# 56 matmuls on half and full rows of the array added behind the preparation of the first keys

## The chip, the cores and the metric

One Trainium2 chip, one core of it in use. The time is device microseconds of one execution of the whole program, from the start to the end of the kernel on that core; the median of several runs is compared.

## The reference

Three stages run one after the other, in fp32, on batch 2, 3008 rows and 256 columns:

```python
scores = (1.0 / S) * np.matmul(z, z.transpose(0, 2, 1))   # z: 2 x 3008 x 64
attn = np.maximum(scores, 0.0) ** 2
x = (u * np.matmul(attn, v)).reshape(B * S, D)            # u, v: 2 x 3008 x 256
h = x @ w_in                                              # 256 -> 2048
P = a[0] + a[1] * h + a[2] * h**2 + a[3] * h**3
Q = 1.0 + np.abs(b[0]) * np.abs(h) + np.abs(b[1]) * h**2
x = (P / (Q + 1e-06)) @ w_out                             # 2048 -> 256
h = x @ w_in2
out = np.maximum(0.01 * h, h) @ w_out2
```

The weights of the first pair arrive as 64-bit floats and are converted on the chip; those of the second pair likewise.

## The kernel before

The 6016 rows are cut into 12 blocks (`blocks`), six for each batch, of 512 query rows (448 in the last of a batch). Attention goes over the keys in pairs of 128: `NPAIR` = 12 steps for a block, 144 steps in all. One step `t` is four matmuls of scores (`scores`, L243), two ScalarE passes (ReLU L245, square L246), two VectorE passes that split the result into a high and a low half (L251, L256), and, two steps later (`DEPTH`), twelve matmuls with the values (`av`, L275). Each tensor that a matmul reads is held as a high part and a low remainder, both in the fp32r form, so that sums of products keep fp32 accuracy. The score matmul uses this in the partition direction: the 64 columns of z are laid twice on the 128 partitions of a key tile, the high part on partitions 0 to 63 and the remainder on 64 to 127.

The order of the work on every engine is the order in which the program issues it (`tc.manual_schedule()`); each engine's queue is in order. `tasks` holds what is issued at which step; step -1 is run ahead of the loop over `t`. In it stand, in this order, the loads of the first 1024 keys (two halves, on SP's and ScalarE's DMA queues), the load of an activation table, `first_z`, and the load and preparation of the first values (`prep_v`, L200 and L201).

`first_z` (L169 to L184) transposes eight tiles of z on TensorE into two PSUM tiles (`pf`, of the tag `acc1`, and `pg`, of the tag `big`, which has two buffers) and makes from them:

- `queries[0]`, a tile of 128 x 2 x 512: plane 0 is the rounded z (L178), plane 1 the remainder (L182);
- `key_chunk(0)`, a tile of 128 x 1024: the rounded half on partitions 0 to 63 (L181 for columns 0 to 511, L183 for 512 to 1023), the remainder on partitions 64 to 127 (L180 and L184).

Behind it TensorE's queue goes on with `scores(0)`, `scores(1)`, the eight transposes of the second 1024 keys (`prep_z`, L153, whose raw data comes by DMA from L129), `scores(2)`, `av(0)`, `scores(3)`, `av(1)` and so on, one `scores` and one `av` in turn. `av(0)` takes the PSUM tile of the tag `acc0`; nothing ahead of it uses that tag.

Each matmul of the program is two instructions on TensorE, a load of 128 x 128 weights and the stream of the moving operand; the trace lists them as PEld and PE.

Of the kernel before, what the change touches and what calls it, by code (L numbers as in the profile page):

```python
# [17 lines left out]
def f32(ap):  # L18
    return ap.bitcast(F32)
# [3 lines left out]
def squared_relu_attention_moe_moe2(  # L23
# [14 lines left out]
    pe, act, dve, pool, sp = nc.tensor, nc.scalar, nc.vector, nc.gpsimd, nc.sync  # L38
# [4 lines left out]
    P = 128  # L43
# [24 lines left out]
    def big(name):  # L68
        return ps.tile([P, 2, QB], F32, tag="big", name=name)

    def acc(k, name):
        return ps.tile([P, 2, QB], F32, tag=f"acc{k}", name=name, bufs=1)
# [4 lines left out]
    def idle_acc(i, name):  # L77
        return acc(1 - own_acc(i), name)
# [39 lines left out]
    queries = [sb.tile([P, 2, QB], F32R, tag="sq", name="sq"), keys[1][:, 1, :].rearrange("p (a b) -> p a b", a=2)]  # L118
# [3 lines left out]
    def key_chunk(c):  # L122
        return keys[c // 2][:, c % 2, :]

    def load_z(b, c, k0=0, k1=8):
        t = raw_slot(f"zraw{b}_{c}_{k0}", (P, 8, 2, DQ))
        f0, f1 = c * 8 + k0, min(c * 8 + k1, S // P)
        for d, queue in enumerate((sp, act if c == 0 else sp)):
            queue.dma_start(t[:, : f1 - f0, d, :], z[b, f0 * P : f1 * P, :].rearrange("(k p) d -> p k d", p=P))  # L129
        if f1 - c * 8 < k1:  # L130
            for h in range(2):
                for d in range(2):
                    sp.dma_start(t[h * KTAIL : (h + 1) * KTAIL, f1 - f0, d, :], z[b, f1 * P : S, :])
        return t
# [16 lines left out]
    def turn_z(pf, t, n):  # L151
        for k in range(n):
            pe.transpose(pf[:, k * P : (k + 1) * P], t[:, k, :, :].rearrange("p a d -> p (a d)"), ident)  # L153
# [15 lines left out]
    def first_z(ts):  # L169
        pf = idle_acc(0, "zT0_0").rearrange("p a b -> p (a b)")  # L170
        pg = big("zT0_0b").rearrange("p a b -> p (a b)")
        m, q = key_chunk(0), queries[0]
        for _ in range(WARM):
            pe.matmul(pg[:, :P], ident, ident, start=True, stop=True)
        turn_z(pf, ts[0], 4)
        for _ in range(2):
            pe.matmul(pg[:, QB : QB + P], ident, ident, start=True, stop=True)
        act.activation(q[:, 0, :], pf[:, :QB], AF.Copy)  # L178
        turn_z(pg, ts[1], 4)
        dve.tensor_tensor(out=m[64:, :QB], in0=pf[64:, :QB], in1=f32(q[64:, 0, :]), op=ALU.subtract)  # L180
        act.activation(m[:64, :QB], f32(q[:64, 0, :]), AF.Copy)  # L181
        dve.tensor_tensor(out=q[:, 1, :], in0=pf[:, :QB], in1=f32(q[:, 0, :]), op=ALU.subtract)  # L182
        act.activation(m[:, QB:], pg[:, :QB], AF.Copy)  # L183
        dve.tensor_tensor(out=m[64:, QB:], in0=pg[64:, :QB], in1=f32(m[64:, QB:]), op=ALU.subtract)  # L184

    def load_v(b, c):
        t = raw_slot(f"vraw{b}_{c}", (P, 4, D))
        k0 = c * 4
        full = min(4, S // P - k0)
        sp.dma_start(t[:, :full, :], v[b, k0 * P : (k0 + full) * P, :].rearrange("(k p) d -> p k d", p=P))  # L190
        if full < 4:
            for h in range(2):
                sp.dma_start(t[h * KTAIL : (h + 1) * KTAIL, full, :], v[b, (k0 + full) * P : S, :])
        return t

    def prep_v(b, c, t):
        m = rtile(3 + c, f"V{b}_{c}")
        V[b, c] = m
        tf = t.rearrange("p k d -> p (k d)")
        act.activation(m[:, 0, :], tf, AF.Copy)  # L200
        dve.tensor_tensor(out=m[:, 1, :], in0=tf, in1=f32(m[:, 0, :]), op=ALU.subtract)  # L201
        if c == KB // 4 - 1:
            o = 3 * D
            act.activation(m[:KTAIL, 1, o:], f32(m[:KTAIL, 0, o:]), AF.Copy)
            pool.memset(f32(m[KTAIL:, 0, o:]), 0.0)
# [145 lines left out]
    def at(step, f):  # L351
        tasks.setdefault(step, []).append(f)
# [3 lines left out]
    def prep(step, lead, key, load, use):  # L356
        at(step - lead, lambda: held.__setitem__(key, load()))
        at(step, lambda: use(held.pop(key)))

    def zt(b, c, step, lead):  # L360
        prep(step, lead, ("z", b, c), lambda: load_z(b, c), lambda t: prep_z(b, c, t, step // NPAIR))

    def zs(b, c, step, lead):
        key = "z", b, c
        at(step - lead, lambda: held.__setitem__(key, load_z_squares(b, c)))
        at(step, lambda: dve.transpose(out=held[key], in_=held[key]))
        at(step + 1, lambda: round_z(c, held[key]))
        at(step + 2, lambda: lower_z(c, held.pop(key)))

    def vt(b, c, step, lead):  # L370
        prep(step, lead, ("v", b, c), lambda: load_v(b, c), lambda t: prep_v(b, c, t))

    NV, NM = KB // 4, KB // 8
    for b in range(B):
        s0 = b * NQ * NPAIR
        if b == 0:
            at(-1, lambda: held.__setitem__("z", [load_z(0, 0, k, k + 4) for k in (0, 4)]))
            at(-1, lambda: act.preload_act_table_set("natural_log_exp_and_others"))
            at(-1, lambda: first_z(held.pop("z")))
            vt(0, 0, -1, 0)  # L380
            zt(0, 1, 1, 2)
            vt(0, 1, 2, 3)
            for c in range(2, NV):
                vt(0, c, 2 * c, 3)
            zs(0, 2, 3, 3)
        else:
            for c in range(NM):
                zs(b, c, s0 + (-8, -4, 3)[c], (13, 11, 3)[c])
            for c in range(NV):
                vt(b, c, s0 - NPAIR + 2 * c + 4, (14, 14, 3, 3, 3, 3)[c])  # L390
# [336 lines left out]
```

## Time and profile before

| what | value |
|---|---|
| median of 2 runs | 1552.22 us (1551.65 and 1552.78) |
| span of the profiled execution | 1550.2 us, first to last instruction |
| TensorE matmul busy | 1542.4 us, 99% of the span |
| weight loads busy | 1297.8 us |
| VectorE busy | 1367.6 us, 88% |
| ScalarE busy | 1067.2 us, 69% |

The profiled execution is given by its span alone; its time is this span and what lies ahead of the first instruction and behind the last, which by the median of the runs is 2.0 us. Busy time of PE is the union of the matmuls' durations, which overlap one another, so a busy PE isn't PE at its peak; the distance between the starts of consecutive matmuls tells more.

### The profile page before, as it was taken

What the parts mean: (1) busy time and instruction counts of PE and PEld (TensorE: products, weight loads), DVE (VectorE), ACT (ScalarE), POOL (GpSimd) and SP (SyncE); (2) the same over time, 40 slices, a digit from 0 to 9 for tenths busy, and PEclk for the clock granted to TensorE, in tenths of its full rate; (3) what the DMA queues carried; (4) which work ended last, traced back from release to release, by engine and by line L of the source; (5) the groups of instructions that cost most, each with busy time, mean ns of one, the idle gap of its engine ahead of it and who ended that gap; (6) DMA issues with size and microseconds to landing.
All of it is one profiled execution on the core that took longest, in us unless ns stands there. A gap on an engine that the chain in (4) does not pass through costs nothing.

```text
span 1550.2 us, 17531 instructions
## 1 busy us (share of the span) xinstructions
PE 1542.4 (99%) x6920; PEld 1297.8 (84%) x6920; DVE 1367.6 (88%) x1301; ACT 1067.2 (69%) x1072; POOL 1.4 (0%) x10
## 2 busy tenths in 40 slices
PE   9999999999999999999999999999999999999998
PEld 7888889888888888888888888888888888888888
DVE  7888889788789899999999998999999999999862
ACT  7666667766677767777667677677776676767653
POOL 0000000000000000000000000000000000000000
PEclk9999999999999999999999999999999999999999
DMA  7332456355410340000000010000000000100001
GB/s 188 84 80 71 108 135 173 82 130 142 109 39 1 121 152 10 14 14 14 14 12 15 1 28 1 14 14 14 13 14 14 14 14 1 22 5 1 14 8 19
DMA packets 144978, 74.41 MB, mean 48 GB/s; under 512 B 121344, under 2 KB 128512, under 8 KB 143872
## 3 DMA queue, kind: packets, MB, share of 16 engines
q1 hardware_dynamic: 141984, 72.80, 18.7%
q8 instruction: 55, 0.90, 0.3%
q10 hardware_dynamic: 2912, 0.49, 0.2%
q14 instruction: 27, 0.22, 0.0%
HBM read 46.93 MB, written 20.71 MB: 44 GB/s over the span
## 4 chain that ended last, share of the span: by engine, by line
PE 97%; DVE 2%; DMA 0%; ACT 0%; issue 0%; SPq 0%; DVEq 0%
PE h L456 33%; PE y L467 32%; PE oT L275 24%; PE sc L243 8%; PE y2b L467 1%; DMA zraw<-in_z_dram 0%; DVE t L499 0%; DVE t L498 0%; DVE pl L256 0%; DVE t L494 0%; DVE t L518 0%; DVE gh L510 0%; DVE t L514 0%; DVE ph L251 0%; SPq L129 0%
## 5 line engine op out<-in xcount | busy, mean ns | idle before, releaser
L467 PE MATMUL y<-gh,w 128*128 128x512 f32 (+1 forms) x1504 | 370.3, 386 | 0.2 <-ACT gh L541 0.2
L467 PEld LDWEIGHTS y<-gh,w 128*128 128x128 f32 x1504 | 282.3, 188 | 53.7 <-ACT gh L541 0.6
L275 PE MATMUL oT<-ph,V 128*128 128x512 f32 (+1 forms) x1128 | 274.7, 385 | 0.0
L275 PEld LDWEIGHTS oT<-ph,V 128*128 128x128 f32 x1128 | 211.7, 188 | 39.8
L467 PE MATMUL y<-gl,w 128*128 128x512 f32 (+1 forms) x752 | 200.1, 386 | 0.1
L484 ACT ACTIVATE t<-h,par 128x1024 f32<-128x1024 f32 (+1 forms) x91 | 100.2, 1101 | 134.9 <-PE h L456 134.9
L541 ACT ACTIVATE gh<-h 128x1024 fp32r<-128x1024 f32 (+1 forms) x96 | 97.0, 1010 | 131.0 <-PE y L467 109.7
L456 PE MATMUL h<-x2h,w 128*128 128x512 f32 (+1 forms) x768 | 186.6, 385 | 0.0
L456 PEld LDWEIGHTS h<-x2h,w 128*128 128x128 f32 x768 | 144.2, 188 | 26.5
L467 PEld LDWEIGHTS y<-gl,w 128*128 128x128 f32 x752 | 141.1, 188 | 27.5 <-DVE gl L548 0.5
L275 PE MATMUL oT<-pl,V 128*128 128x512 f32 (+1 forms) x576 | 151.6, 385 | 0.0
L548 DVE TENSOR_TENSOR gl<-g,gh 128x1024 fp32r<-128x1024 f32 (+1 forms) x96 | 114.9, 1197 | 30.2 <-ACT g L543 30.2
L494 DVE SCALAR_TENSOR_TENSOR t<-t,par,t 128x1024 f32<-128x1024 f32 (+1 forms) x91 | 114.2, 1255 | 29.0 <-ACT t L487 28.9
L503 ACT ACTIVATE t<-t,par 128x1024 f32<-128x1024 f32 (+1 forms) x91 | 103.3, 1135 | 47.2 <-DVE t L494 47.2
L456 PE MATMUL h<-x,w 128*128 128x512 f32 (+1 forms) x576 | 133.9, 381 | 0.7 <-DVE t L499 0.7
L245 ACT ACTIVATE r<-sc 128x1024 f32<-128x1024 f32 (+1 forms) x96 | 96.4, 1004 | 46.2 <-PE sc L243 45.0
L510 DVE SCALAR_TENSOR_TENSOR gh<-t,par,t 128x1024 fp32r<-128x1024 f32 (+1 forms) x91 | 114.7, 1260 | 12.3 <-DVE t L499 1.0
L275 PEld LDWEIGHTS oT<-pl,V 128*128 128x128 f32 x576 | 108.1, 188 | 20.2
L456 PEld LDWEIGHTS h<-x,w 128*128 128x128 f32 x576 | 108.0, 188 | 19.5 <-PE y L467 1.1
L256 DVE TENSOR_TENSOR pl<-r,ph 128x1024 fp32r<-128x1024 f32 (+1 forms) x96 | 115.5, 1203 | 9.7 <-PE oT L275 0.9
L518 DVE SCALAR_TENSOR_TENSOR t<-t,par,t 128x1024 f32<-128x1024 f32 (+1 forms) x96 | 121.1, 1262 | 3.1
L499 DVE SCALAR_TENSOR_TENSOR t<-t,par,h 128x1024 f32<-128x1024 f32 (+1 forms) x96 | 120.9, 1259 | 3.4
(88 smaller groups left out, 2146.5 us busy)
## 6 DMA issues: line engine op xcount, KB each, us to landing
wraw<-in_moe_w_in_dram SPq DMA_DIRECT2D x16, 512.0 KB, 4.6
wraw<-in_moe_w_out_dram SPq DMA_DIRECT2D x16, 512.0 KB, 4.2
w2s<-wst SPq DMA_DIRECT2D x16, 512.0 KB, 3.7
w<-w2s SPq DMA_DIRECT2D x8, 1024.0 KB, 4.8
vraw<-in_v_dram SPq DMA_DIRECT2D x10, 512.0 KB, 5.0
u<-in_u_dram SPq DMA_DIRECT2D x40, 128.0 KB, 4.3
xs<-u SPq DMA_DIRECT2D x10, 512.0 KB, 5.1
out_dram<-yo SPq DMA_DIRECT2D x40, 128.0 KB, 3.2
```

The lines of the kernel that those rows point to most:

```text
L243: pe.matmul(s[:, e, :n], m, queries[i % 2][:, h, :n], start=h == 0, stop=h == 1)
L256: dve.tensor_tensor(out=pl, in0=r, in1=f32(ph), op=ALU.subtract)
L275: pe.matmul(a[:, j, :n], vt[:, h, o : o + P], mv[:, e, :], start=pr == 0 and si == 0 and e == 0, stop=pr == NPAIR - 1 and si == 2 and e == 1)
L456: pe.matmul(h[:, e, :n], w[:, hl, o : o + P], mv[:, k, :n], start=si == 0 and k == 0, stop=si == 2 and k == 1)
L467: pe.matmul(a[j], w[:, hl, o : o + P], mv[:, e, :], start=p == 0 and si == 0 and e == 0, stop=p == NP - 1 and si == 2 and e == 1)
L484: act.activation(T[c]["t1"], T[c]["h"], AF.Abs, scale=b0)
L494: dve.scalar_tensor_tensor(out=d["t2"], in0=d["t2"], scalar=b1, in1=d["t1"], op0=ALU.mult, op1=ALU.add)
L499: dve.scalar_tensor_tensor(out=d["t3"], in0=d["t3"], scalar=ca[1], in1=d["h"], op0=ALU.add, op1=ALU.mult)
L503: act.activation(d["t1"], d["t2"], AF.Ln, scale=LSH, bias=lnb)
L510: dve.scalar_tensor_tensor(out=m1_tile(c, "gh", 14, F32R), in0=d["t3"], scalar=ca[0], in1=d["t1"], op0=ALU.add, op1=ALU.mult)
L518: dve.scalar_tensor_tensor(out=d["t3"], in0=d["t3"], scalar=ca[0], in1=d["t2"], op0=ALU.add, op1=ALU.subtract)
L548: dve.tensor_tensor(out=d["gl"], in0=d["g"], in1=f32(d["gh"]), op=ALU.subtract)
```

## The change

One function is new and is called once, at step -1, behind `first_z` and ahead of the first values. It takes a PSUM tile of the tag `acc0` (two banks of 512 columns) and issues 56 matmuls of 512 moving columns into it. `rows(r, e, k, h)` multiplies the key columns `k` (128 of them) of the partitions `r` with the queries of the same partitions into bank `e`. Every one begins a sum of its own and ends it, and nothing reads the tile. The four parts are: 12 pairs, one on partitions 0 to 63 into bank 0 and one on 64 to 127 into bank 1; 6 groups of a full one (128 partitions, bank 0) and such a pair; 6 full ones in turn on the two banks; 8 on partitions 0 to 63, all into bank 0. That is 24 + 18 + 6 + 8 = 56, of which 44 read half of the partitions and 12 all.

```diff
+    def half_rows():
+        m, q = key_chunk(0), queries[0]
+        t = acc(0, "rows")
+        top, bottom = slice(0, 64), slice(64, P)
+
+        def rows(r, e, k, h=0):
+            pe.matmul(t[:, e, :], m[r, k * P : (k + 1) * P], q[r, h, :], start=True, stop=True)
+
+        for k in range(12):
+            rows(top, 0, k % 8)
+            rows(bottom, 1, k % 8)
+        for k in range(6):
+            rows(slice(0, P), 0, k)
+            rows(top, 0, k)
+            rows(bottom, 1, k)
+        for k in range(6):
+            rows(slice(0, P), k % 2, k)
+        for k in range(8):
+            rows(top, 0, k)
...
             at(-1, lambda: first_z(held.pop("z")))
+            at(-1, half_rows)
             vt(0, 0, -1, 0)
```

## Rows read from the trace of the kernel before

**Rows 1.** The page, its head and part 1: busy time of each engine.

```profile
span 1550.2 us, 17531 instructions
...
PE 1542.4 (99%) x6920; PEld 1297.8 (84%) x6920; DVE 1367.6 (88%) x1301; ACT 1067.2 (69%) x1072; POOL 1.4 (0%) x10
```

**Rows 2.** All waits of PE over the span: total us, times, longest.

```profile
PE zT_0b L174 <- POOL ident masks.py:199: 1.4, 1, 1.4
PE h L456 <- DVE t L499: 0.7, 1, 0.7
PE sc L243 <- DVE keys L180: 0.5, 1, 0.5
PE zT L153 <- DMA zraw<-in_z_dram: 0.4, 1, 0.4
PE y L467 <- ACT gh L541: 0.2, 1, 0.2
```

**Rows 3.** Chain that ended last: start, length, work; from stretches 0:30 and whole span.

```profile
2.90 6.57 DMA zraw<-in_z_dram
9.47 0.14 issue
9.60 1.06 PE zT L153 x8
10.67 0.93 PE sc L243 x4
11.60 2.76 PE oT L275 x12
14.36 0.91 PE sc L243 x4
...
579.64 3.63 PE y L467 x16
```

**Rows 4.** Timeline of the first 14 us, weight loads: start, length, merged, count, idle before.

```profile
6.65 0.30 PEld L243 LDWEIGHTS sc<-sq,keys 128*128 128x128 f32 x2 [0.72 <-ACT keys L181]
...
8.04 0.77 PEld L243 LDWEIGHTS sc<-sq,keys 128*128 128x128 f32 x4 [0.43 <-DVE keys L184]
...
9.57 0.86 PEld L153 LDWEIGHTS zT<-ident,zraw 128*128 128x128 f32 x8 [0.77 <-issue]
```

**Rows 5.** Timeline of PE's matmuls in the same stretch.

```profile
6.68 2.55 PE L243 MATMUL sc<-sq,keys 128*128 128x512 f32 x8 [0.51 <-DVE keys L180]
...
10.42 1.18 PE L243 MATMUL sc<-sq,keys 128*128 128x512 f32 x4
11.44 2.02 PE L275 MATMUL oT<-ph,V 128*128 128x512 f32 x8
```

**Rows 6.** The same stretch, ScalarE and VectorE.

```profile
5.84 0.63 ACT L181 ACTIVATE keys<-sq 64x512 fp32r<-64x512 f32 x1
...
7.29 0.69 DVE L184 TENSOR_TENSOR keys<-zT_0b,keys 64x512 fp32r<-64x512 f32 x1
...
7.43 1.06 ACT L200 ACTIVATE V<-vraw 128x1024 fp32r<-128x1024 f32 x1 [0.48 <-DMA vraw<-in_v_dram]
...
8.39 1.01 ACT L245 ACTIVATE r<-sc 128x1024 f32<-128x1024 f32 x1
...
10.52 0.69 DVE L251 CAST ph<-r 128x1024 fp32r<-128x1024 f32 x1 [0.78 <-ACT r L246]
```

**Rows 7.** Groups by line and shape, 10 to 300 us: busy us, mean ns.

```profile
L243 PE MATMUL sc<-sq,keys 128*128 128x512 f32 x184 | 49.3, 390 | 0.0
...
L243 PEld LDWEIGHTS sc<-sq,keys 128*128 128x128 f32 x184 | 34.5, 188 | 7.0
```

**Rows 8.** Stretches: length, busy us (count) of each engine, granted clock, DMA.

```profile
4.00:6.65 2.65, 2.17 (x14) 1.93 (x13) 0.78 (x2) 1.41 (x3) 0.00 (x0) 1.00 1.09 286
6.65:10.00 3.35, 2.95 (x12) 1.70 (x13) 2.53 (x3) 2.84 (x4) 0.00 (x0) 1.00 1.01 236
20.00:30.00 10.00, 10.00 (x46) 8.29 (x45) 9.42 (x10) 8.93 (x11) 0.00 (x0) 1.00 0.52 136
```

## The prediction

> **What bounds the kernel now.** I read the page first: matmuls are busy for 99% of the span [rows 1]. Busy time of overlapping matmuls can hide gaps, so the next view is the list of waits. All waits of PE together are 3.2 us, and three of the five entries (1.4, 0.5 and 0.4 us) lie in the first 10 us [rows 2]. The chain that ended last confirms it: from 9.60 us on it runs on PE with scores and value matmuls back to back [rows 3]. So TensorE's issue rate sets the time, and whatever is put into its queue at the start delays the rest, unless it fills a wait that is there already.
>
> The rate is the number that everything below rests on. The chain has 16 matmuls in 3.63 us [rows 3], which is 0.2269 us from start to start. One such matmul is recorded with 0.390 us, and its weight load with 0.188 us [rows 7], so about 0.163 us of each matmul lie under the next one, and the loads are hidden. I use 0.227 us for a full matmul of 512 columns.
>
> The start is different, and its order matters. The first score matmul starts at 6.68 us, when the upper keys of columns 0 to 511 are there (L181: 5.84 + 0.63 = 6.47 us) [rows 5, 6]. Eight score matmuls would need 8 x 0.227 = 1.82 us, but the next work, the transposes of the second keys, starts only at 9.60 us, released by the DMA of their raw data [rows 2, 3]: 2.92 us pass where 1.82 are worked. From first score matmul to first value matmul it is 11.44 - 6.68 = 4.76 us [rows 5]. This stretch alone can give something back.
>
> **The change, part by part.** It removes and moves nothing. It adds no DMA and no work on ScalarE, VectorE, GpSimd or SP. It adds 56 matmuls with their weight loads to TensorE's queue between the transposes of `first_z` and `scores(0)`, and one wait inside them. The PSUM tile is of the tag `acc0`, first used by `av(0)` on the same engine in order, and nothing reads it, so I cost the tile at nothing; if a release between the two tiles were to cost a semaphore, it would be one, of the size of the issue gap of 0.14 us in the chain [rows 3].
>
> *The wait.* The pair with k = 4 reads the second half of the key columns. Its lower rows come from L184, which ends at 7.29 + 0.69 = 7.98 us [rows 6], and the first load behind that very instruction in the kernel before started at 8.04 us [rows 4]. I let the lower matmul of that pair start at 8.07 us. Behind it in TensorE's queue stand all other added matmuls and everything that follows; no other engine has work until `scores(0)`, apart from the first values (L200, L201), which depend on a DMA alone.
>
> *A pair.* The trace of before has no matmul on 64 rows, so its price is bounded from both sides. If the halves stream side by side, a pair costs what one full matmul does, 0.227 us; if one follows the other, 0.454 us. Less than 0.227 is excluded, since each half still streams 512 columns. Could the loads stand in the way of the lower end? The eight transposes have eight loads of the same 128 x 128 size in 0.86 us [rows 4], 0.108 us each at most; the two loads of a pair are then 0.215 us, just within 0.227. The halves read different partitions and write different banks, and the load of one half needn't wait for the other half to be done. I take 0.227 us, the end to which the loads' row gives room, with no great trust.
>
> The page "TensorEngine Tiling (Array Packing)" of the Trainium skill, section Key Properties, says that different tiles of the array can load and multiply in parallel, which would give the lower end; no row here shows it.
>
> *A change between full and half.* After a pair, a full matmul needs rows that both halves still use. The lower bound is nothing, as between full ones. An upper bound for the drain is the part of a matmul that lies under the next one, 0.390 - 0.227 = 0.163 us; if the weight load is exposed too, add 0.188 us, 0.351 in all [rows 7]. A gain is excluded, since no order makes a stream shorter. I count the changes: in each of the 6 groups one from half to full and one back makes 12; into the 6 full ones, into the 8 upper ones and out into `scores(0)` makes 3 more. The first pair follows a wait anyway. 15 x 0.163 = 2.45 us; 15 x 0.351 = 5.27 us. I take the drain alone, since in the steady state the loads are hidden.
>
> The same section of that page of the Trainium skill states that changing the tiling mode drains the engine, which speaks against this change; with it the sum gets the 2.45 us, without it nothing, and the trace of before can't show which.
>
> *The sum, pairs side by side.* Pairs k = 0 to 3: 6.68 + 4 x 0.227 = 7.59 us, then the wait to 8.07. Eight more pairs: 8.07 + 8 x 0.227 = 9.89. Six groups, each a full one and a pair: 12 x 0.227 = 2.72, to 12.61. Six full ones: 1.36, to 13.97. Eight upper ones, which share their rows and so go one by one: 1.82, to 15.79. With the changes 15.79 + 2.45 = 18.24 us. There `scores(0)` can start, against 6.68 before: 11.56 us later.
>
> *What comes back.* The raw keys for the transposes, and the first values, are there long before. So TensorE could be at the first value matmul after 8 scores, the transposes (0.86) and 4 scores: 12 x 0.227 + 0.86 = 3.58 us after `scores(0)` starts. But `av(0)` needs the chain behind the first scores: their fourth matmul starts 0.68 us in and lasts 0.39, then ReLU to first value matmul is 11.44 - 8.39 = 3.05 us [rows 5, 6]; with 0.03 for the handover this makes 4.15 us. Before it was 4.76, because ScalarE was in the first values' copy (L200, 7.43 + 1.06 = 8.49) and the transposes waited. So 4.76 - 4.15 = 0.61 us come back, and a new wait of 0.57 us shows ahead of `av(0)`. Bounds: 0 and 4.76 - 3.58 = 1.18 us. Later waits (0.7 and 0.2 us [rows 2]) hang on the pipeline itself, and move along.
>
> Total: 11.56 - 0.61 = **10.95 us**. On the profiled span that is 1550.2 + 10.95 = 1561.2; the median of the runs lies 2.0 us above that span, so the prediction is 1552.22 + 10.95 = **1563.2 us**, 0.7% more.
>
> **The rivals.** *Side by side, changes free.* Only the 2.45 us fall away: 8.5 us, **1560.7**. It differs from the forecast in one term.
>
> *One after the other.* The array takes one matmul at a time whichever rows it reads. For it: all matmuls of before start in order, one by one, at an even distance. Against it: only that the halves share neither rows nor banks. 56 x 0.227 = 12.71 us, the wait for L184 disappears under the first eight (6.68 + 1.82 = 8.50), less 0.61: 12.1 us, **1564.3**. With drains at the changes 14.55 us, **1566.8**; with exposed loads as well 17.4 us, **1569.6**.
>
> *The added work is hidden or absent.* As nothing reads the results, they might not be in the program that runs; then **1552.2**. The profile counts 6920 matmuls before [rows 1], so it would tell at once. As for hiding: the room at the start is the 1.18 us above, so even the cheapest order can't vanish.
>
> *The other side: TensorE's clock falls (slower by over 2%).* The granted clock is 1.00 in the stretches that I read, at the start with its gaps too [rows 8], so 2.4 GHz. If matmuls on half of the rows made the chip grant 1.2 GHz, every period would double: the 56 would cost 25.4 us in place of 12.71, which gives 24.8 us with what comes back, **1577**. The bound of 2% is 31 us; the missing 6.2 us are reached when the low clock stays for 12.4 us of the attention behind it, in which some 27 matmuls run. Against it: no stretch of before shows the low level, whatever TensorE did there [rows 8].
>
> **How the numbers follow.** The forecast, pairs side by side with a cost at the changes, gets 0.42; side by side with free changes 0.18; one after the other in its three prices 0.32; hidden or absent 0.03; the clock 0.03, of which 0.02 lie beyond 2%; 0.02 for something else. The range leaves out the absent, the clock, and the dearest of one after the other: from 1559.5 (free changes, with the whole 1.18 us coming back, and 0.6 us for the spread of the runs) to 1568.0 (one after the other with drains, with nothing coming back and the same spread). Within 2%, which is about what a measurement of this kernel can tell from no change, lie all cases but the clock: 0.97; faster 0.01, slower 0.02.
>
> **What would show it.** The profile after should have 6976 matmuls. In the timeline of PE the added group starts near 6.7 us; its 12 pairs end near 9.9 us if side by side, near 12.1 if one after the other. The groups of three then last 0.454 us each with free changes, 0.78 with drains, 0.68 one after the other, and the last eight 1.82 us in each case. `scores(0)` starts near 18.2 us. The list of waits should lose the ones on L180's keys for the scores and on the raw keys' DMA, and gain one of about 0.6 us on ScalarE or VectorE ahead of `av(0)`; everything from `av(0)` on should be displaced by the same 11 us up to the end, with the granted clock still 1.00. The prediction is wrong if the displacement isn't constant (then a second engine matters), if the wait for L184 reaches past 8.1 us, or if changes between full and half rows cost more than a drain and a load.

## The result and the profile after

The changed kernel took 1564.11 us (1564.09 and 1564.13), against 1552.22 before: ratio 1.0076, 95% interval 1.0059 to 1.0092. That is 11.9 us more by the medians and 12.1 by the spans; forecast were 10.95 us and 1563.2. It lies inside the range of 1559.5 to 1568.0, but so do the prices of most rivals, and it is within 0.2 us of the first price of one of them (one after the other, 1564.3). The total alone doesn't tell them apart.

The page's head and part 1, the changed kernel. The 56 matmuls are there (6976 against 6920 [rows 1]), and no other engine has more work:

```profile
span 1562.3 us, 17642 instructions
...
PE 1555.2 (100%) x6976; PEld 1305.5 (84%) x6976; DVE 1367.4 (88%) x1301; ACT 1066.9 (68%) x1072; POOL 1.4 (0%) x10
```

Timeline of its weight loads: start, length of the merged stretch, what, how many, and idle time before it in brackets:

```profile
6.92 1.05 PEld L192 LDWEIGHTS rows<-sq,keys 64*128 64x128 f32 x9 [0.33 <-ACT keys L181]
8.41 1.68 PEld L192 LDWEIGHTS rows<-sq,keys 64*128 64x128 f32 x15 [0.44 <-DVE keys L184]
10.44 0.19 PEld L192 LDWEIGHTS rows<-sq,keys 128*128 128x128 f32 x1 [0.35 <-issue]
10.87 0.19 PEld L192 LDWEIGHTS rows<-sq,keys 64*128 64x128 f32 x2 [0.25 <-issue]
11.31 0.19 PEld L192 LDWEIGHTS rows<-sq,keys 128*128 128x128 f32 x1 [0.25 <-issue]
...
15.62 1.24 PEld L192 LDWEIGHTS rows<-sq,keys 128*128 128x128 f32 x6 [0.25 <-issue]
17.22 1.68 PEld L192 LDWEIGHTS rows<-sq,keys 64*128 64x128 f32 x8 [0.36 <-issue]
19.26 1.69 PEld L263 LDWEIGHTS sc<-sq,keys 128*128 128x128 f32 x8 [0.36 <-issue]
```

Three things are to be read here. **The pairs run side by side.** 15 loads of halves from 8.41 us on take 1.68 us, as long as the eight loads of halves without a partner at 17.22. They lie in twos: two loads that would take 0.188 us each share one stretch of 0.19 us ("x2" at 10.87). **A change between full and half rows has a price.** From 10.44 to 10.87 and on to 11.31 it is 0.43 us each, where streams without a change follow at 0.227; ahead of each load PEld is idle for 0.25 us. **The eight upper ones** take 1.68 us for eight loads, as eight full ones do in the last row: without a partner a half costs a full one.

The granted clock over the six groups of a full one and a pair (length, busy us and count of PE, PEld, DVE, ACT and POOL, granted clock, DMA):

```profile
10.40:15.60 5.20, 5.20 (x19) 2.23 (x18) 0.00 (x0) 0.00 (x0) 0.00 (x0) 1.00 0.85 148
```

Timeline of its matmuls, start and length of each merged stretch on PE:

```profile
5.93 1.06 PE L153 MATMUL zT_0b<-ident,zraw 128*128 128x128 f32 x4
6.92 12.41 PE L192 MATMUL rows<-sq,keys 64*128 64x512 f32 x56
19.26 2.11 PE L263 MATMUL sc<-sq,keys 128*128 128x512 f32 x8
21.21 1.03 PE L153 MATMUL zT<-ident,zraw 128*128 128x128 f32 x8
22.00 1.17 PE L263 MATMUL sc<-sq,keys 128*128 128x512 f32 x4
23.39 2.10 PE L295 MATMUL oT<-ph,V 128*128 128x512 f32 x8 [0.22 <-DVE ph L271]
```

The scores start at 19.26 us, where 18.24 was forecast and 6.68 was before [rows 5]. From there to the first value matmul it is 4.13 us, against 4.76 before. The list of PE's waits has lost the two that were expected to go [rows 2] and gained the one ahead of `av(0)`:

```profile
PE zT_0b L174 <- POOL ident masks.py:199: 1.4, 1, 1.4
PE h L477 <- DVE t L520: 0.7, 1, 0.7
PE oT L295 <- DVE ph L271: 0.2, 1, 0.2
PE y L488 <- ACT gh L562: 0.2, 1, 0.2
```

Behind that nothing is added. The chain that ended last has the work of the last row of [rows 3] at

```profile
591.69 3.63 PE y L488 x16
```

which is 12.05 us later than before; the first value matmul is 11.95 us later (23.39 against 11.44). The displacement made in the first 24 us is carried to the end.

### The profile page after: what moved, and what is told of

Same layout as the page of the kernel before. It is cut to its first block, busy times and chain, and to the rows that moved or that the text cites. A ratio compares the mean times of both kernels' runs of the same rounds, so it can differ in the third digit from the quotient of the medians.

```text
span 1562.3 us, 17642 instructions
## 1 busy us (share of the span) xinstructions
PE 1555.2 (100%) x6976; PEld 1305.5 (84%) x6976; DVE 1367.4 (88%) x1301; ACT 1066.9 (68%) x1072; POOL 1.4 (0%) x10
## 4 chain that ended last, share of the span: by engine, by line
PE 97%; DVE 2%; ACT 0%; issue 0%; POOL 0%; DVEq 0%; POOLq 0%
PE h L477 32%; PE y L488 32%; PE oT L295 23%; PE sc L263 8%; PE rows L192 1%; PE y2b L488 1%; DVE t L520 0%; DVE t L519 0%; DVE pl L276 0%; PE zT_0b L174 0%; DVE t L515 0%; DVE t L539 0%; DVE gh L531 0%; DVE t L535 0%; DVE ph L271 0%
## 5 line engine op out<-in xcount | busy, mean ns | idle before, releaser
L531 DVE SCALAR_TENSOR_TENSOR gh<-t,par,t 128x1024 fp32r<-128x1024 f32 (+1 forms) x91 | 114.7, 1260 | 12.3 <-DVE t L520 1.0
```

Source lines behind the costliest of these rows:

```text
L531: dve.scalar_tensor_tensor(out=m1_tile(c, "gh", 14, F32R), in0=d["t3"], scalar=ca[0], in1=d["t1"], op0=ALU.add, op1=ALU.mult)
```

## The experiments

All of them change the added matmuls alone, and nothing reads their results. Differences are against the median of the kernel before on the same chip.

**e1_full56: no half at all.**

```diff
-        (the four parts)
+        for k in range(56):
+            rows(slice(0, P), k % 2, k // 2 % 8)
```

> The added work is replaced by 56 full matmuls on the two banks in turn; results not read. Theory (halves stream side by side, and each change between full and half rows costs about 0.21 us): full ones go one by one at 0.227 us and none changes the mode, so 12.7 us of stream, less 0.6 us that come back: +12.1 us, close to the change's own time although it holds no pair. Rival (halves go one after the other and changes cost nothing): the same +12.1 us in total, so the total can't tell them apart here, but weight loads should then be spaced in the groups of the change as here, at 0.227 us each; the theory wants 0.43 us there and 0.227 us here.

Measured: 1564.24 us against 1551.94, +12.3, ratio 1.0079 (1.0062 to 1.0096). Its weight loads in the timeline:

```profile
6.64 12.56 PEld L192 LDWEIGHTS rows<-sq,keys 128*128 128x128 f32 x56 [0.65 <-ACT keys L181]
```

56 loads without a break in 12.56 us, 0.22 us each. So 56 plain full matmuls cost what the change costs. What the pairs of the change save, its changes of rows take back.

**e2_pairs28: pairs alone.**

```diff
+        for k in range(28):
+            rows(top, 0, k % 8)
+            rows(bottom, 1, k % 8)
```

> 28 pairs on the upper and lower 64 rows, no full one among them; results not read. Theory: 28 x 0.228 = 6.4 us, about 0.5 us of wait for the lower keys, one change out of the half rows 0.2 us, less 0.6 us that come back: +6.5 us. Rival (one after the other): 56 x 0.227 less 0.6 = +12.1 us.

Measured: 1558.55, +6.6 us, ratio 1.0043 (1.0028 to 1.0058). The loads:

```profile
6.43 0.98 PEld L192 LDWEIGHTS rows<-sq,keys 64*128 64x128 f32 x9 [0.70 <-ACT keys L181]
7.95 5.33 PEld L192 LDWEIGHTS rows<-sq,keys 64*128 64x128 f32 x47 [0.53 <-DVE keys L184]
13.63 1.69 PEld L255 LDWEIGHTS sc<-sq,keys 128*128 128x128 f32 x8 [0.35 <-issue]
```

The loads lie in twos here too. Here a two is the lower half of one pair and the upper half of the next. The end of the 47, eleven twos and the last load, which is alone:

```profile
10.60 2.68 PEld L192 LDWEIGHTS rows<-sq,keys 64*128 64x128 f32 x23
```

From two to two that is (2.68 - 0.18) / 11 = 0.227 us, the price of one full matmul. One after the other would have been +12.1. That rival falls.

**e3_turns28: a change at every matmul.**

```diff
+        for k in range(28):
+            rows(slice(0, P), 0, k % 8)
+            rows(top, 1, k % 8)
```

> 28 times a full matmul and one on the upper rows, each in its own bank, so 56 matmuls and 56 changes; results not read. Theory (a change costs 0.21 us on top of the stream, in either direction): 56 x 0.434 = 24.3 us, less 0.6: +23.7 us. Rival A (a change is a drain alone, 0.163 us): 56 x 0.390 = 21.8, +21.2 us. Rival B (drain and load one after the other, 0.351 us): 56 x 0.578 = 32.4, +31.8 us. Rival C (the spacing of the groups of three came from the pair in them, not from the change): 56 x 0.227, +12.1 us.

Measured: 1575.33, 1575.39, 1584.86 and 1590.36 us, median +28.2, ratio 1.019 (1.0147 to 1.0234). The two shortest are at +23.4, where the theory had +23.7; drain alone (+21.2), drain plus load (+31.8) and a change for nothing (+12.1) are off. The two others come with something that no theory here had expected, a lower granted clock: its mean over the run is 0.988 and 0.992 in them, 0.999 and 1.000 in the two shortest. Stretches of the profiled one (1590.36 us), by length, busy us and count of each engine, granted clock, DMA:

```profile
6.50:11.20 4.70, 4.70 (x12) 2.03 (x12) 2.38 (x3) 1.21 (x2) 0.00 (x0) 1.00 1.19 234
11.40:43.40 32.00, 32.00 (x45) 12.59 (x44) 0.00 (x0) 0.00 (x0) 0.00 (x0) 0.50 0.15 42
43.50:48.50 5.00, 5.00 (x16) 4.12 (x16) 0.75 (x2) 2.90 (x3) 0.00 (x0) 0.50 0.00 0
49.00:60.00 11.00, 11.00 (x50) 9.06 (x49) 10.50 (x11) 9.38 (x10) 0.00 (x0) 1.00 0.39 116
```

And loads of the same run at either level:

```profile
7.21 0.19 PEld L192 LDWEIGHTS rows<-sq,keys 128*128 128x128 f32 x1 [0.25 <-issue]
7.64 0.18 PEld L192 LDWEIGHTS rows<-sq,keys 64*128 64x128 f32 x1 [0.24 <-issue]
...
20.31 0.29 PEld L192 LDWEIGHTS rows<-sq,keys 128*128 128x128 f32 x1 [0.44 <-issue]
21.03 0.28 PEld L192 LDWEIGHTS rows<-sq,keys 64*128 64x128 f32 x1 [0.44 <-issue]
```

At 1.00 (2.4 GHz) a matmul with the change ahead of it takes 0.43 us, at 0.50 (1.2 GHz) 0.72. The low level lasts into the scores, and is over at 49 us.

**e4_middle: the same 56 in the third block.**

```diff
-        t = acc(0, "rows")
+        t = idle_acc(2, "rows")
...
-            at(-1, half_rows)
+            at(28, half_rows)
```

`idle_acc(2, ...)` is the PSUM tile that the third block doesn't use for its values.

> The 56 matmuls of the change, unaltered, in the third block of attention (step 28) in place of the start; results not read. Theory (TensorE sets the time there too, without a wait and without anything that comes back): 38 streams of 0.228 us and 16 changes of 0.207 us, 8.66 + 3.31 = +12.0 us, with no gap of TensorE behind it. Rival (the start has a price of its own that isn't the matmuls': its wait, its restart of the chain behind the first scores): here less by these, +11 us or under; or (ScalarE and VectorE fall behind) a gap behind the group and +13 us or more.

Measured: 1563.98, +12.04 us, ratio 1.0077 (1.0062 to 1.0093). In its timeline of PE the group lies between matmuls without an idle time in brackets. From the start of the last four value matmuls to the scores it is 12.78 us, and without those four (0.91) 11.87:

```profile
106.58 1.07 PE L295 MATMUL oT<-pl,V 128*128 128x512 f32 x4
107.58 11.85 PE L192 MATMUL rows<-sq,keys 64*128 64x512 f32 x56
119.36 1.20 PE L263 MATMUL sc<-sq,keys 128*128 128x512 f32 x4
120.40 1.98 PE L295 MATMUL oT<-ph,V 128*128 128x512 f32 x8
```

The sum from 0.228 per stream and 0.207 per change, 12.0 us, holds where the trace shows no wait and no gap. At the start a wait and what comes back about cancel.

**e5_turns10, e6_turns10_w72, e7_turns10_256: what a change consists of.** The three have 20 matmuls in turn, `for k in range(10)` in the loop of e3; e6 and e7 change `rows` as well:

```diff
 e6
-            pe.matmul(t[:, e, :], m[r, k * P : (k + 1) * P], q[r, h, :], start=True, stop=True)
+            pe.matmul(t[:72, e, :], m[r, k * P : k * P + 72], q[r, h, :], start=True, stop=True)
 e7
+            pe.matmul(t[:, e, :256], m[r, k * P : (k + 1) * P], q[r, h, :256], start=True, stop=True)
```

> 10 times a full matmul and one on the upper rows, so 20 matmuls and 20 changes, as a base for the next two runs; results not read. Theory L (at a change the next weights are loaded only when the stream before is over, so the load is exposed): spacing 0.432 us as in the 28 turns at the full clock, 20 x 0.432 = 8.6, less 0.6: +8.0 us. Theory D (the array drains, and the load is hidden): the same here, as the spacing is already measured. Granted clock 1.00: both expect it, but the 28 turns fell to 0.50 after five us in one of their runs; if that happens here, the time rises by up to 3 us.

> The 10 turns with 72 of the 128 weight columns, streams of 512 columns unaltered; results not read. Theory L: the exposed load gets shorter, by the 56 columns that are left out at 0.108 us for 128 (the spacing of the eight transposes' loads) 0.047 us, or if all of its 0.187 us go with the columns 0.082 us; spacing 0.35 to 0.385, +6.4 to +7.1 us. Theory D: a drain doesn't depend on the load, spacing 0.432, +8.0 us.

> The 10 turns with streams of 256 columns in place of 512, weights unaltered; results not read. Theories L and D both (a fixed price for a change of 0.205 us): the stream gets shorter by 256 columns, 0.107 us by the full clock's 0.2269 for 512 less the part that doesn't go with columns; spacing 0.325, +5.9 us. Rival P (a change costs in proportion to the stream, because the next one waits for a whole recorded matmul): spacing 0.216, +3.7 us.

Measured: e5 1562.50, +10.4 (1560.35 to 1563.80), ratio 1.0065 (1.0050 to 1.0080); e6 1559.11, +7.0 (1558.94 to 1559.42), 1.0045 (1.0029 to 1.0062); e7 1561.01, +8.9 (1559.81 to 1561.68), 1.0056 (1.0041 to 1.0071). In the profiled runs of e5 and e7 the granted clock fell again. Stretches of e5, then of e7:

```profile
13.50:20.00 6.50, 6.50 (x13) 3.85 (x13) 0.00 (x0) 1.32 (x2) 0.00 (x0) 0.50 0.59 166
```

```profile
9.70:14.90 5.20, 5.20 (x11) 2.86 (x10) 0.00 (x0) 0.00 (x0) 0.00 (x0) 0.50 0.87 122
```

So the totals of these two miss the expected +8.0 and +5.9 and aren't the test. The one run of e5 with a mean clock of 0.999 (1560.35, +8.2) fits; e7 has none, all four lie at 0.997 or 0.998. The test is the loads at 1.00, of e5, of e6 and of e7:

```profile
10.08 0.19 PEld L192 LDWEIGHTS rows<-sq,keys 128*128 128x128 f32 x1 [0.25 <-issue]
10.51 0.18 PEld L192 LDWEIGHTS rows<-sq,keys 64*128 64x128 f32 x1 [0.24 <-issue]
10.93 0.19 PEld L192 LDWEIGHTS rows<-sq,keys 128*128 128x128 f32 x1 [0.24 <-issue]
```

```profile
8.04 0.14 PEld L192 LDWEIGHTS rows<-sq,keys 128*72 128x72 f32 x1 [0.24 <-issue]
8.42 0.14 PEld L192 LDWEIGHTS rows<-sq,keys 64*72 64x72 f32 x1 [0.24 <-issue]
8.80 0.14 PEld L192 LDWEIGHTS rows<-sq,keys 128*72 128x72 f32 x1 [0.24 <-issue]
```

```profile
6.65 3.02 PEld L192 LDWEIGHTS rows<-sq,keys 128*128 128x128 f32 x10 [0.29 <-ACT keys L181]
```

With 72 weight columns the load goes from 0.19 to 0.14 us, the idle time ahead of it stays 0.24, and the distance from load to load goes from 0.43 to 0.38. So the load stands in the period with its whole length: theory L, and +7.0 is the upper of its two figures. A drain that hides the load (D) would have left 0.43. With 256 columns ten loads take 3.02 us, (3.02 - 0.19) / 9 = 0.314 from start to start: 0.12 less than with 512, which is about the stream's own shortening. A price in proportion to the stream (P) would have been 0.216.

**e8_groups18: the second part of the change, three times as long.**

```diff
+        for k in range(18):
+            rows(slice(0, P), 0, k % 8)
+            rows(top, 0, k % 8)
+            rows(bottom, 1, k % 8)
```

> 18 groups of a full matmul and a pair in place of all 56 of the change, so its second part three times as long, 54 matmuls and 36 changes; results not read. Theory (the group's price is the measured 0.865 us, and the granted clock stays at 1.00 as in the change): 15.6 less 0.6, +15.0 us, the runs within half a microsecond. Rival (changes kept up for longer let the granted clock fall to 0.50, as in the 28 turns, where a change and stream took 0.723 us): +18 to +25 us in some runs, and the runs apart by microseconds. Rival (one after the other): 0.68 us per group, +11.6 us.

Measured: 1567.14 (1566.92 to 1567.19), +15.0 us, ratio 1.0096 (1.0081 to 1.0111). The expected +15.0 holds to a tenth. The granted clock over the group:

```profile
6.50:22.00 15.50, 15.49 (x54) 6.67 (x54) 2.51 (x3) 1.34 (x2) 0.00 (x0) 1.00 0.70 158
```

**e9_pairs4: is a small addition hidden?** Four pairs (`for k in range(4)` in the loop of e2).

> Only the first four pairs (columns 0 to 511, so no wait for the rest of the keys); results not read. Theory (0.6 us of what is added at the start come back): four pairs 0.91 us and one change 0.21, less 0.6: +0.5 us. Rival A (nothing comes back, the price is all of TensorE's time): +1.1 us. Rival B (the room at the start, 2.92 us where 1.82 are worked, takes all of it): 0.

Measured: 1552.61 against 1551.92, +0.7 us, ratio 1.0004 (0.9995 to 1.0014). The interval holds all three answers, so the times don't decide. In the profile the scores start at 7.71 us and the first value matmul at 11.87, 4.16 us later:

```profile
7.71 2.14 PE L255 MATMUL sc<-sq,keys 128*128 128x512 f32 x8
9.71 1.06 PE L153 MATMUL zT<-ident,zraw 128*128 128x128 f32 x8
...
11.87 2.12 PE L287 MATMUL oT<-ph,V 128*128 128x512 f32 x8 [0.17 <-DVE ph L263]
```

The first value matmul is 0.43 us later than before [rows 5], although the scores are 1.03 us later. This one profile speaks for the 0.6 us that come back.

**e10_upper56: halves without a partner.**

```diff
+        for k in range(56):
+            rows(top, k % 2, k // 2 % 8)
```

> 56 matmuls on the upper rows alone, on the two banks in turn; results not read. Theory (without a partner a half costs what a full one does; one change at the end): 56 x 0.227 + 0.21 - 0.6 = +12.3 us at a granted clock of 1.00. Rival A (a stream on half of the rows is shorter): below +11. Rival B (half of the array idle lets the granted clock fall, as in the 28 turns): +18 us or more in some runs, and the runs apart.

Measured: 1564.40 (1564.26 to 1565.00), +12.5 us, ratio 1.0081 (1.0068 to 1.0095), with the granted clock at 1.00 from 7.6 to 24 us and a mean of 0.999 or 1.000 in each of the four runs. A half alone costs what a full one does. Rival A falls, and B didn't show.

## Why the prediction was right, and where a term was off

**What bounds the kernel:** right. TensorE's issue rate does; 12 us put into its queue came out as 12 us at the end, at the start (+11.9) and in the third block (+12.04).

**The pairs:** right, 0.227 us (e2), the lower end of the two bounds. The argument for it was only half right: I checked that two loads fit one after the other into a pair's time (2 x 0.108). The trace shows that they don't follow each other; both lie in the same 0.19 us. That the halves stream side by side was a choice between two bounds "with no great trust", and came out.

**The changes:** mis-sized, and taken for the wrong thing. The prediction took 0.163 us for a drain with the load hidden "since in the steady state the loads are hidden". Measured were 0.205 to 0.207 us on top of the stream (a group of the change lasts 11.31 - 10.44 = 0.87 us, less 2 x 0.227 that is 0.41 for two; in the turns of e5 0.43 - 0.227). e6 shows what it is: the load is not hidden, and its 0.187 us are nearly all of the price. A load for other rows starts only when the stream before is about over (the idle 0.24 us are little more than the 0.227 of a stream), and the stream behind waits for it. Drain and load don't add up to the 0.351 of the upper bound. 15 x (0.207 - 0.163) = 0.66 us were missing in the sum. The page that the prediction names, "TensorEngine Tiling (Array Packing)" of the Trainium skill, says under Key Properties that a change of mode drains the engine; the trace agrees in that the load at a change isn't hidden under a stream (0.19 of the 0.43 us). Its other rule there, tiles in parallel, agrees with e2 (0.227 us a pair).

**The wait inside the group:** the mechanism was right, the place off by 0.34 us. The load behind L184 started at 8.41 us, not 8.07. This is one of the signs that the prediction gave for being wrong (the wait reaches past 8.1 us). Nothing of the change lies ahead of it; the transposes of `first_z` were slower in this profile. Four of them took 1.06 us (5.93 us in the timeline above); in the profile of e2 the same four, timeline of PE, were at

```profile
5.37 0.60 PE L153 MATMUL zT_0b<-ident,zraw 128*128 128x128 f32 x4
```

and L184 followed at 7.20 instead of 7.66 us. The instructions are the same. The slow four aren't the change's doing: e4, which has no added work at the start, had them too.

```profile
5.82 1.06 PE L153 MATMUL zT_0b<-ident,zraw 128*128 128x128 f32 x4
```

Their length is that of the low level of the clock. Groups of transposes with their mean ns: the four after, the four of e2, and eight of e3 in its stretch at 0.50:

```profile
L153 PE MATMUL zT_0b<-ident,zraw 128*128 128x128 f32 x4 | 1.1, 421 | 0.0
L153 PE MATMUL zT_0b<-ident,zraw 128*128 128x128 f32 x4 | 0.6, 273 | 0.0
L153 PE MATMUL zT<-ident,zraw 128*128 128x128 f32 x8 | 1.9, 420 | 0.0
```

The views print 1.00 for this stretch, but they print that also where the trace has no record of the clock. Its first record, at the full level, begins at 7.07 us after, at 6.84 in e4 and at 4.87 in e2. In each of the twelve profiles the four take 0.60 us where that record begins ahead of them (seven), 1.06 where it begins within 0.1 us of their end or behind it (three), and 0.78 and 0.92 where it begins in their midst (two). So the 1.00 in the first of [rows 8] isn't a reading of the clock up to 5.30 us, where the record of the kernel before begins. Why the full level comes at another time in each run stays open.

**What comes back:** right, 4.76 - 4.13 = 0.63 us for 0.61, with a wait of 0.2 us on L271 in the list of PE (0.66 us for its weight loads) for the 0.57 forecast.

Together: 18.24 + 0.34 + 0.66 = 19.24 us for the start of the scores, measured 19.26. The two terms add 1.0 us to 10.95, and the spans gave 12.1. They have the same sign, so the forecast's nearness doesn't come from errors that cancel.

**The rivals.** One after the other had the better total (+12.1) and the wrong mechanism: 18 pairs save 18 x 0.227 = 4.1 us, 15 changes cost 15 x 0.207 = 3.1 us, and the wait for the lower keys, which this rival doesn't have, costs 0.8 (8.41 against 7.59 us). 12.1 - 4.1 + 3.1 + 0.8 is 11.9; that the two totals agree is chance. e2 (+6.6) settles it. The added work isn't absent (6976). The clock didn't fall in the change: it is 1.00 from 10.4 to 15.6 us, the two runs are 0.04 us apart, and e8, with 36 changes of the same kind, stayed at 1.00.

## What to carry to other kernels

Two matmuls on separate halves of the rows, with separate PSUM banks, run for the price of one, but only among themselves: going into such a stretch and out of it costs 0.21 us each, almost a full matmul of 512 columns. A pair saves 0.227 us, so a stretch needs two pairs to pay for its two changes (0.41 us), and more to gain. For the scores of this kernel, four full ones a step between value matmuls, three pairs, if they could stand in place of the four, would save 0.227 us and cost 0.41 in each step; this is an estimate from the rows above, and it wasn't tried, nor were pairs that write the same bank. And when two theories give the same total, as here within 0.2 us, change the mix of the work (e2) before believing either.

## What the runs showed of the hardware that was not expected

The granted clock fell to 0.50 within a stretch in which TensorE had no wait, in e3 from between 11.2 and 11.4 us to between 48.5 and 49 us. It fell in the profiles of e5 and e7 too. By the mean clock of each run it fell in two of the four runs of e3 (0.988 and 0.992), three of e5 (0.996 and 0.997) and all four of e7 (0.997 and 0.998), against 0.999 or 1.000 in all others. What preceded the falls was a full matmul and a single upper one in turn, with 128 weight columns. It stayed at 1.00 with 72 weight columns (e6), with full ones and pairs in turn (e8), with upper ones alone (e10, on another chip than e3, e5 and e7), and in the change. The prediction's rival of the falling clock is thus real, with a price here of up to 15 us (1590.36 - 1575.33), though not under the conditions that it named.

Its price per matmul holds for full ones. Timeline of PE in e3 at 0.50, the scores and the transposes behind them:

```profile
43.45 3.78 PE L255 MATMUL sc<-sq,keys 128*128 128x512 f32 x8
47.03 1.91 PE L153 MATMUL zT<-ident,zraw 128*128 128x128 f32 x8
```

That is (47.03 - 43.45) / 8 = 0.45 us for one, twice 0.227; a matmul with a change takes 0.72 in place of 0.43. Against this rival the prediction said that no stretch of before shows the low level. One that it didn't show does: the end of the kernel, 1540 to 1552 us, has 0.84, with TensorE busy for 5.65 us of it. What sets the falls off within unbroken work stays open.
